# Attention scores in four 64x64 parts of the array, AV's copies on VectorE, and a replanned order

## The chip, the cores and the metric

The kernel runs on one core of one Trainium2 chip. The metric is device time in microseconds of one execution; less is better. The core's engines work from queues of their own: PE (TensorE matmuls; PEld are its weight loads), ACT (ScalarE), DVE (VectorE), POOL (GpSimd), and SP, which here only starts DMAs. They meet through semaphores.

## The reference, cut to what matters

Sliding window attention with four sink keys, 4 batches, 8 heads, 768 positions, head size 64, and behind it a mixture of experts that takes each token once:

```python
scores = q @ k.T / sqrt(64)
keep = (key < 4) | ((query - key >= 0) & (query - key < 128))
a = softmax(where(keep, scores, -1e9))
x = (a @ v)                       # [3072 tokens, 512]
# MoE: 8 experts, 384 tokens each, assigned greedily by x @ w_gate
out[tokens of e] = relu(x @ w1[e]) @ w2[e]
```

All is float32.

## The kernel before, in words

**Chunks.** Attention works in 24 chunks of 128 queries (`c`; `i = c % 6` is the block within a batch), each with all 8 heads as four pairs. The two heads of a pair lie in partitions 0 to 63 and 64 to 127 of `q` and `k`. A query sees the keys of its own block up to itself, those of the block before from itself on (exclusive), and the four sinks: 128 window keys and four sinks for every query.

**One chunk's operations** (each a function `op_...` of `attention`; a digit is the pair or the half):
- `QK0` to `QK3` (L68 to L74, PE): scores of one pair, for both heads `s`; 128 queries against 260 columns: 128 keys of the block before, the block's four sinks (copied in front of it in `kk`), 128 keys of the block. In the first block (`i = 0`) there are 132 columns, and no block before. Each float32 matmul shows in the trace as two passes.
- `cp` (L75 to L81, DVE, `copy_predicated`): overwrites the scores of the block's keys that lie behind the query with those of the block before for the same position, which are exactly the keys that the window lets through there; in the first block with -1e9. In the second block (`i = 1`) one more small copy (L80) masks sinks that are already in the window. After it, 132 columns hold all that counts.
- `mx` (L84, DVE): negated maximum over the 132 columns. `e` (L89, ACT): exponential with that bias, and its sum read out.
- `T0`, `T1` (L95, PE): transposes of the 128 window columns, `pe` (L96, ACT): copy of them to SBUF, `A`, `B` (L97, L98, POOL): the part that belongs to the block itself and to the block before.
- `ss`, `Ts`, `pS` (L100, L104, L105): the sink columns gathered, transposed, copied.
- `AV0`, `AV1` (L112, PE): values by probabilities, two pairs each, 32 instructions in a chunk (16 in a first block); both heads of a pair go to two halves of the columns of the array. `ae0`, `ae1` (L115, ACT): copies of AV from PSUM to `at`.
- `X0`, `X1` (L121, L124, PE): sinks' part, and `at` transposed back with the gate's logits beside it; `xe` (L126, DVE) scales by the sums' reciprocals (`ra`, `r`), `lm` (L128, DVE) adds the logits, `xo` (SP) stores x.

**Shapes on PE.** QK, T, Ts and X use 64 rows by 128 columns of the array (`64*128` in the trace), in two halves of the rows side by side; AV uses `128*64`, two halves of the columns.

**Buffers.** Four PSUM tiles `pp` of two banks each are shared by QK, T, Ts, AV, X; a QK's tile is free after its exponentials, AV's after both `ae`.

**What sets the order.** Nothing is scheduled on the chip. `schedule` (L220) is a list planner that runs on the host when the kernel is built: `table` gives each operation its engine, a cost in ns and its inputs; `buffers` says what must be free; `SWITCH` adds a cost when PE goes from one kind of operation to another (`c` is AV, `n` is U, `r` the rest); a priority is chunk number times a period plus the operation's `OFF`. `plan` turns the result into one sequence, and `attention` emits it in that order, so each engine's queue has that order. Loads of q and k for the chunk four ahead are started behind QK3, those of v behind QK2, the store behind `xe`, all on SP. POOL scales q (`qs`).

**Ahead and behind.** Seven matmuls on zeros (L48) warm the clock while the first loads run. After attention come routing (from L506, L530: small matmuls and DVE chains), then the expert layers; they are not touched.

Of the kernel before, what the change touches and what calls it, by code (L numbers as in the profile page):

```python
# [7 lines left out]
AF=mybir.ActivationFunctionType; OP=mybir.AluOpType; AX=mybir.AxisListType  # L8
# [7 lines left out]
def attention(ctx,tc,qd,kd,vd,vs,ud,iwd,ident,idn,x_dram,L,side={}):  # L16
# [16 lines left out]
    def T(tag,c,op=None): return R[tag][pl['slot'][tag,op or tag,c]]  # L33
# [11 lines left out]
    m1=mprev[:,0:4]  # L45

    pp=[ps.tile([128,2,512],F32,name=f"pp{j}") for j in range(bn['p'])]
    for i in range(7): PE.matmul(pp[0][:,0],wz[:,0:128],wz,start=True,stop=True)  # L48
    R.update(p=pp)

    sst=[[tl([128,2,B,HP,4],f"ss{b}_{j}") for j in range(bn['ss'])] for b in range(B)]
# [15 lines left out]
    def op_qs(c,h=slice(0,HP),e=G): e.tensor_scalar(qs[c%NQ][:,h],qs[c%NQ][:,h],0.125,None,op0=OP.mult)  # L67
    def op_QK(c,g):  # L68

        i=c%NB; q=qs[c%NQ]; sp=T('p',c,f'QK{g}')  # L70
        k0=(i-1)*W+4 if i else 0; n=260 if i else 132
        for s in range(2):
            p=slice(64*s,64*s+64)
            PE.matmul(sp[:,s,:n],q[p,g,:],kk[p,g,k0:k0+n],start=True,stop=True)  # L74
    def op_cp(c,g):  # L75

        i=c%NB; sp=T('p',c,f'QK{g}')
# [34 lines left out]
                    PE.matmul(av[64*s:64*s+64,hp-2*g,:],T('v',j)[:,h*64:h*64+64],T(x,c)[:,h,:],start=hp==2*g and x=='A',stop=x=='B' or not i,skip_group_check=True)  # L112
    def op_ra(c): V.tensor_scalar(T('r',c),T('sm',c),1e-9,None,op0=OP.add)
    def op_r(c): V.reciprocal(T('r',c),T('r',c))
    def op_ae(c,g): A.activation(T('at',c)[:,2*g:2*g+2],T('p',c,'AV0')[:,g,0:256].rearrange("p (j n)->p j n",j=2),AF.Copy)  # L115
    def op_X(c,g):

        xp=T('p',c,'X0')
# [46 lines left out]
def table(cfg):  # L165
    o={}
    def add(k,e,c,deps,alloc=()): o[k]=(e,c,deps)
    f0=lambda x: lambda c: x if c==0 else None
    f1=lambda x: lambda c: None if c==0 else x
    for p in range(3): add(f'qs.{p}','V',f0((195,195,260)[p]),[(f'ldq{p}',0)])  # L170
    add('qs','P',lambda c: 1450 if c else None,[('ldq',0)])
    for h in range(4):
        add(f'QK{h}','E',lambda c: 435 if c%NB else 225,[('ldk',0),('ldk',-1),('qs',0),(f'qs.{min(h,2)}',0),(f'ldk{min(h,2)}',0)])
        add(f'cp{h}','V',lambda c: 550 if c%NB==1 else 345,[(f'QK{h}',0)])
        add(f'mx{h}','V',344,[(f'cp{h}',0)])
        add(f'e{h}','A',697,[(f'mx{h}',0)])
    ae=[(f'e{h}',0) for h in range(4)]
    for g in range(2):
        add(f'T{g}','E',440,[(f'e{2*g}',0),(f'e{2*g+1}',0),('ldn',0)])
        add(f'pe{g}','A',479,[(f'T{g}',0)])  # L180
        add(f'A{g}','P',596,[(f'pe{g}',0)])
        add(f'B{g}','P',lambda c: 596 if c%NB else None,[(f'pe{g}',0)])
    add('zs','P',lambda c: 480 if c%NB==1 and c//NB<B-1 else None,[('A1',0)])
    add('ss','A',130,ae+[('~zs',1-NB)])
    add('ra','V',75,ae)
    add('r','V',120,[('ra',0)])
    add('Ts','E',115,[('ss',0),('ldn',0)])
    add('pS','A',230,[('Ts',0)])
    add('U','E',f0(860),[('ldu',0)])
    add('Uc','A',f0(160),[('U',0)])  # L190
    add('um','V',f0(120),[('Uc',0),('ldS',0)])
    for g in range(2):
        add(f'AV{g}','E',lambda c,g=g: 870 if c%NB else 435,
            [(f'A{g}',0),(f'B{g}',0),('ldV',0),('ldV',-1)]+([] if g==0 else [('AV0',0)]))
        add(f'ae{g}','A',285,[(f'AV{g}',0)])
    add('X0','E',950,[('ae0',0),('pS',0),('um',0),('ldi',0)])
    add('X1','E',460,[('X0',0),('ae1',0)])
    add('xe','V',680,[('X1',0),('r',0)])
    add('lm','V',135,[('xe',0)])
    add('xo','S',0,[('xe',0)])  # L200

    add('fi','P',lambda c: 500 if 2<=c<8 else None,[('A1',0)])
    last={'L':'lm'}
    for j,(cost,rd,wr) in enumerate(PREP):
        add(f'pr{j}','V',lambda c,cost=cost: cost if c==AHEAD else None,[(last[x],0) for x in rd.split() if x in last and x!='L']+([('ldn',0),('lm',-1),('lm',-2),('lm',-3)] if j==0 else []))
        last[wr]=f'pr{j}'
    return o
# [12 lines left out]
def schedule(cfg,off,T,nb=NC,dl={}):  # L220
# [63 lines left out]
    while len(out)<total:  # L284
        best=None
        for e,a in avail.items():
            cand=[]
            for p,k,c in a:
                s=max(et[e],ready[k,c]); ok=True
                for t,g in alltag.get(k,()):  # L290
                    if (t,g,c) in got: continue
                    f=free[t]
                    if not f: ok=False; break
                    if f[0][0]>s: s=f[0][0]
                if ok: cand.append((s,p,k,c))
            if not cand: continue
            m=min(cand)[0]
            x=min((p,s,k,c) for s,p,k,c in cand if s<=m+WIN)
            if best is None or x[1]<best[0]: best=(x[1],e,x[0],x[2],x[3])
        if best is None: return None  # L300
        s,e,p,k,c=best
        avail[e].remove((p,k,c))
        cost=o[k][1]; cost=cost(c) if callable(cost) else cost
        skip=cost is None
        if skip: s=ready[k,c]; t1=s
        else:
            t1=s+cost
            if e=='E':
                md='c' if k[:2]=='AV' else 'n' if k=='U' else 'r'
                t1+=SWITCH.get(mode[0]+md,0); mode[0]=md  # L310
            if e=='E' and s<60000 and s-et[e]>400:
                fr=[('p',x[1]) for x in free['p'] if x[0]<=et[e]]
                if fr: fills.append((et[e]+1,(fr[-1],int((s-et[e]-150)//(216 if et[e]>3420 else 430)))))
            if e!='S': et[e]=t1
        out.append((s,k,c,t1,skip))
        for t,g in alltag.get(k,()):
            if (t,g,c) not in got:
                got.add((t,g,c)); f=free[t]; j=0
                while j+1<len(f) and f[j+1][0]<=s: j+=1
                slot[t,g,c]=f.pop(j)[1]  # L320
        resolve(k,c,t1,skip)
        released(k,c,t1+200)
        if k=='AV1' or k[:2]=='QK':
            if c and c%NB: released(k+'+',c-1,t1+200)
            if c%NB==NB-1: released(k+'+',c,t1+200)
        if k=='xo': t=trig(t1,'xo',c); released('xod',c,dma(t+100,1456))
        if k=='QK3':
            n=c+AHD
            if n<nb:
                t=trig(t1,'ldk',n); resolve('ldk',n,dma(t,Q)); t=trig(t,'ldq',n); resolve('ldq',n,dma(t,Q))  # L330
        if k=='QK2' and c: t=trig(t1,'lv',c); resolve('ldV',c,dma(t,750))
    return max(x[3] for x in out),out,ld+[(t,'fill',f) for t,f in fills],slot
SOLO={'p'}
SWITCH=dict(rc=250,cr=200,nc=200,cn=150,nr=90,rn=200)
def plan_of(res,cfg):
    ms,out,ld,slot=res
    ev=[(s,2,k,c) for s,k,c,t,sk in out if not sk and k!='xo']+[(t,1,k,c) for t,k,c in ld]
    ev.sort(key=lambda x:x[:3])
    sl={((t,g,c) if t in SOLO else (t,t,c)):j for (t,g,c),j in slot.items()}
    return dict(seq=[(k,c) for _,_,k,c in ev],slot=sl,bufs={t:n for t,(n,_) in buffers(cfg).items()})  # L340
OFF={'A0': 117339, 'A1': -133923, 'AV0': 12422, 'AV1': -21208, 'B0': 10595, 'B1': 259267, 'QK0': -22052, 'QK1': -14777, 'QK2': -13749, 'QK3': -6157, 'T0': 4670, 'T1': -246750, 'Ts': 2621, 'U': 152873, 'Uc': -95211, 'X0': 17495, 'X1': -104106, 'ae0': 2467, 'ae1': -31194, 'cp0': 278259, 'cp1': -108689, 'cp2': 87460, 'cp3': 64960, 'e0': -138537, 'e1': -108673, 'e2': -114256, 'e3': -23766, 'fi': 109507, 'lm': -139787, 'mx0': -116627, 'mx1': -231823, 'mx2': 124490, 'mx3': 5320, 'pS': -115720, 'pe0': -173530, 'pe1': -184, 'pr0': 159594, 'pr1': -86684, 'pr10': 59638, 'pr11': -60475, 'pr12': 217358, 'pr13': -126818, 'pr14': 80178, 'pr15': 130654, 'pr2': -40108, 'pr3': -132402, 'pr4': -221748, 'pr5': 217675, 'pr6': -82969, 'pr7': 10706, 'pr8': -58787, 'pr9': 116352, 'qs': 14397, 'r': 10669, 'ra': -56880, 'ss': 189502, 'um': 89415, 'xe': 45272, 'xo': -27345, 'zs': -53942, 'pr16': 130654}
PCFG={'win': 80}
def plan():
    cfg=PCFG
    return plan_of(schedule(cfg,OFF,11557.5,dl=DL),cfg)
DL={}

I16=mybir.dt.int16; F16=mybir.dt.float16
# [7 lines left out]
class Graph:  # L356

    def __init__(self): self.t=[]; self.lw={}; self.rd={}
    def add(self,e,cost,fn,r=(),w=(),name='',cls='',lat=None):
        i=len(self.t); dep={}  # L360
        def on(j,war=False):
            if j is None: return
            pe=self.t[j][0]
            l=0 if war and pe==e else ML.get(pe+e,200) if lat is None or war else lat
            dep[j]=max(dep.get(j,0),l)
        for x in r: on(self.lw.get(x))
        for x in w:
# [440 lines left out]
```

## Time and profile before

| | |
|---|---|
| median of 3 runs | 534.67 us (530.03 to 535.22) |
| the profiled execution's own time | 532.35 us |
| its span, first to last instruction | 530.6 us |
| its mean granted TensorE clock | 0.958 of full speed |
| busy, share of the span | PE 92%, PEld 76%, DVE 66%, ACT 47%, POOL 29% |

How to read the rows below: times are us from the span's start unless said otherwise. In a timeline a row is one run of like instructions: its start, how long until the last of them ended, engine, line of the kernel, operation, output and inputs by name, partitions x elements, how many; a bracket gives idle time of the engine just before, and what ended it. A matmul's end is modelled and includes the way through the array, so starts tell more than durations: the distance between the starts of two neighbours on PE is what one costs in a stream. "Who waited for whom" puts a wait down to the releaser that came last.

### The profile page before, as it was taken

The numbers are of one execution on the slowest core, as the hardware profiler recorded it, in microseconds if no ns is written. First come the engines' busy times: TensorE is split into PE (matmuls) and PEld (weight loads), VectorE is DVE, ScalarE is ACT, GpSimd is POOL, SyncE is SP. The second block draws the span as 40 slices with busy tenths as digits, with TensorE's granted clock in tenths as the row PEclk, the third lists the DMA queues.
The fourth block names the chain that finished last, engine by engine and source line by source line (L and its number), as shares of the span: only waits on it lengthen the run. The fifth ranks groups of instructions, "written<-read, shape, count | busy, mean of one in ns | idle before, by whom it ended". The sixth has DMA issues, their size and how long they took to land. (4 is left out here: it accounts for less than half of the span.)

```text
span 530.6 us, 11127 instructions
## 1 busy us (share of the span) xinstructions
PE 487.3 (92%) x3999; PEld 404.7 (76%) x3999; DVE 350.1 (66%) x1112; ACT 248.7 (47%) x714; POOL 152.0 (29%) x207
## 2 busy tenths in 40 slices
PE   6999999999995497999989999989999989999994
PEld 4687787787873267868868977868878868999983
DVE  3766767777676686787787897877788765642100
ACT  4788887888860053153153163162055155442110
POOL 4767665665550030041032030040031041210011
PEclk8999999999997589998998999998999999999998
DMA  7566665566321171291092281380183386610001
GB/s 238 159 195 175 179 184 169 162 171 168 89 59 40 64 255 60 78 318 43 22 324 91 65 272 62 120 298 21 35 283 110 117 251 238 198 61 20 21 34 45
DMA packets 74934, 72.87 MB, mean 137 GB/s; under 512 B 28032, under 2 KB 57472, under 8 KB 74880
## 3 DMA queue, kind: packets, MB, share of 16 engines
q1 hardware_dynamic: 71040, 59.58, 36.7%
q0 software_dynamic: 3840, 12.59, 6.7%
q8 instruction: 31, 0.51, 0.4%
q14 instruction: 23, 0.19, 0.1%
HBM read 59.57 MB, written 12.58 MB: 136 GB/s over the span
## 5 line engine op out<-in xcount | busy, mean ns | idle before, releaser
L639 ACT ACTIVATE wh<-raw 128x1024 fp32r<-128x1024 f32 x64 | 67.6, 1059 | 94.9 <-DMA raw<-w 60.5
L641 DVE TENSOR_TENSOR wl<-raw,wh 128x1024 fp32r<-128x1024 f32 x64 | 77.7, 1219 | 33.2 <-ACT wh L639 32.6
L667 PE MATMUL ph<-xh,wh 128*128 128x384 f32 x256 | 92.4, 361 | 3.5 <-DVE hl L671 3.5
L667 PE MATMUL ph<-xh,wl 128*128 128x384 f32 x256 | 86.5, 338 | 0.0
L667 PE MATMUL ph<-xl,wh 128*128 128x384 f32 x256 | 86.5, 338 | 0.0
L670 ACT ACTIVATE hh<-ph 128x384 fp32r<-128x384 f32 x64 | 31.1, 489 | 104.3 <-PE ph L667 74.2
L679 PE MATMUL py<-wh,hh 128*128 128x512 f32 x192 | 79.7, 415 | 0.1
L684 POOL DMA_INDIRECT out<-yo,idx x24 | 28.5, 1189 | 176.9 <-ACT yo L682 117.3
L679 PE MATMUL py<-wh,hl 128*128 128x512 f32 x192 | 76.7, 399 | 0.4 <-DVE hl L671 0.4
L679 PE MATMUL py<-wl,hh 128*128 128x512 f32 x192 | 76.4, 398 | 0.0
L89 ACT ACTIVATE P<-pp,nmx 128x132 f32<-128x132 f32 x192 | 69.2, 369 | 9.3 <-DVE nmx L84 7.6
L646 POOL DMA_INDIRECT xg<-x_dram,idx x24 | 28.4, 1183 | 134.0 <-PE py L679 68.4
L74 PE MATMUL pp<-kk,q 64*128 64x260 f32 (+1 forms) x384 | 58.4, 403 | 1.4 <-issue 0.6
L671 DVE SCALAR_TENSOR_TENSOR hl<-ph,hh 128x384 fp32r<-128x384 f32 x64 | 35.1, 552 | 35.0 <-ACT hh L670 34.3
L667 PEld LDWEIGHTS ph<-xh,wh 128*128 128x128 f32 x256 | 49.2, 192 | 7.8 <-DVE hl L671 5.1
L79 DVE COPY_PREDICATED pp<-mprev,pp 128x256 f32<-128x256 int32 x80 | 34.0, 424 | 26.5 <-PE pp L104 16.5
L667 PEld LDWEIGHTS ph<-xl,wh 128*128 128x128 f32 x256 | 48.6, 190 | 1.8
L667 PEld LDWEIGHTS ph<-xh,wl 128*128 128x128 f32 x256 | 48.4, 189 | 0.0
L97 POOL TENSOR_SCALAR_AFFINE_SELECT A<-PT 128x512 f32<-128x512 f32 x48 | 31.1, 647 | 48.8 <-ACT PT L96 48.8
L679 PEld LDWEIGHTS py<-wh,hl 128*128 128x128 f32 x192 | 36.6, 191 | 9.0 <-DVE hl L671 0.8
L679 PEld LDWEIGHTS py<-wh,hh 128*128 128x128 f32 x192 | 37.0, 193 | 7.9 <-issue 2.7
L84 DVE TENSOR_REDUCE nmx<-pp 128x2 f32<-128x264 f32 x96 | 40.8, 429 | 1.5
(146 smaller groups left out, 843.3 us busy)
## 6 DMA issues: line engine op xcount, KB each, us to landing
raw<-w SPq DMA_DIRECT2D x64, 512.0 KB, 5.0
v<-vd SPq DMA_DIRECT2D x24, 256.0 KB, 3.6
x_dram<-xt SPq DMA_DIRECT2D x24, 256.0 KB, 3.0
kk<-kd SPq DMA_DIRECT2D x23, 264.0 KB, 3.8
q<-qd SPq DMA_DIRECT2D x23, 256.0 KB, 4.1
xg<-x_dram,idx POOLq DMA_INDIRECT x24, 4.7
out<-yo,idx POOLq DMA_INDIRECT x24, 3.2
us<-ud SPq DMA_DIRECT2D x1, 288.0 KB, 4.2
```

Of the source, the lines that this page charges most:

```text
L74: PE.matmul(sp[:,s,:n],q[p,g,:],kk[p,g,k0:k0+n],start=True,stop=True)
L79: V.copy_predicated(sp[:,:,132:260],mprev[:,None,:].to_broadcast([128,2,128]),sp[:,:,0:128])
L84: V.tensor_reduce(T('nmx',c)[:,2*g:2*g+2],sp[:,:,o:o+132],AX.X,OP.max,negate=True)
L89: A.activation(T('P',c)[:,h,:],sp[:,s,o:o+132],AF.Exp,bias=T('nmx',c)[:,h:h+1],scale=1.0,accum_out=T('sm',c)[:,h:h+1])
L97: def op_A(c,g): G.affine_select(T('A',c)[:,4*g:4*g+4],T('PT',c)[:,4*g:4*g+4],[[0,4],[1,128]],OP.is_ge,0.0,base=0,channel_multiplier=-1)
L639: g.add('A',947,lambda wh=wh,raw=raw: nc.scalar.activation(wh,raw,AF.Copy),[f'raw{n%4}'],[f'wh{s}'],f'H{k}.{j}',f'W{k}')
L641: g.add(e,{'V':1135,'P':2303}[e],lambda wh=wh,wl=wl,raw=raw,e=e: (nc.vector if e=='V' else nc.gpsimd).tensor_tensor(wl,raw,wh.bitcast(F32) ...
L667: nc.tensor.matmul(p[:,0:CAP],x[:,c,:],y[:,c,:],start=c==0 and i==0,stop=c==3 and i==2)
L670: g.add('A',371,lambda f=f,p=p: nc.scalar.activation(self.hh[:,f,:],p[:,0:CAP],AF.Relu),ps,[f'hh{f}'],f'hh{k}.{f}',f'H{k}')
L671: g.add('V',469,lambda f=f,p=p: nc.vector.scalar_tensor_tensor(self.hl[:,f,:],p[:,0:CAP],0.0,self.hh[:,f,:].bitcast(F32),op0=OP.max,op1=OP ...
L679: nc.tensor.matmul(p,x[:,f,ts],w,start=f==0 and i==0,stop=f==7 and i==2)
L684: st=nc.gpsimd.indirect_dma_start(out=self.out,out_offset=bass.IndirectOffsetOnAxis(ap=idx[:,t:t+1],axis=0),in_=y,in_offset=None)
```

## The change

Four things change. The scores of a pair are computed in two halves of the queries: queries 0 to 63 against columns 0 to 196 and queries 64 to 127 against columns 64 to 260 (in a first block 0 to 68, and 0 to 132). What is left out are keys behind every query of the half, and keys that have left the window for all of them, which `cp` overwrites or never takes. Each matmul then has 64 rows and 64 columns of the array, and the two halves and the two heads lie in four different parts. `ae` becomes a copy on VectorE. The planner's costs of QK, T, Ts, X and `ae` are new, it prices QK (`q`) as a kind of its own, and all priorities `OFF` and the period are new, so it plans another order. The warming matmuls are eight and go over all eight PSUM banks.

```diff
-    for i in range(7): PE.matmul(pp[0][:,0],wz[:,0:128],wz,start=True,stop=True)
+    for i in range(8): PE.matmul(pp[i//2][:,i%2],wz[:,0:128],wz,start=True,stop=True)
...
         k0=(i-1)*W+4 if i else 0; n=260 if i else 132
-        for s in range(2):
-            p=slice(64*s,64*s+64)
-            PE.matmul(sp[:,s,:n],q[p,g,:],kk[p,g,k0:k0+n],start=True,stop=True)
+        for h,(a,b) in enumerate(((0,n-64),(64 if i else 0,n))):
+            for s in range(2):
+                p=slice(64*s,64*s+64); r=slice(64*h,64*h+64)
+                PE.matmul(sp[r,s,a:b],q[p,g,r],kk[p,g,k0+a:k0+b],start=True,stop=True)
...
-    def op_ae(c,g): A.activation(T('at',c)[:,2*g:2*g+2],T('p',c,'AV0')[:,g,0:256].rearrange("p (j n)->p j n",j=2),AF.Copy)
+    def op_ae(c,g): V.tensor_copy(T('at',c)[:,2*g:2*g+2],T('p',c,'AV0')[:,g,0:256].rearrange("p (j n)->p j n",j=2))
...
-        add(f'QK{h}','E',lambda c: 435 if c%NB else 225,[...])
+        add(f'QK{h}','E',lambda c: 340 if c%NB else 190,[...])
-        add(f'T{g}','E',440,[...])
+        add(f'T{g}','E',350,[...])
-    add('Ts','E',115,[('ss',0),('ldn',0)])
+    add('Ts','E',65,[('ss',0),('ldn',0)])
-        add(f'ae{g}','A',285,[(f'AV{g}',0)])
-    add('X0','E',950,[...])
-    add('X1','E',460,[...])
+        add(f'ae{g}',cfg.get('ae','A'),{'A':268,'V':335}[cfg.get('ae','A')],[(f'AV{g}',0)])
+    add('X0','E',905,[...])
+    add('X1','E',420,[...])
...
-                md='c' if k[:2]=='AV' else 'n' if k=='U' else 'r'
+                md='c' if k[:2]=='AV' else 'n' if k=='U' else 'q' if k[:2]=='QK' else 'r'
...
-SWITCH=dict(rc=250,cr=200,nc=200,cn=150,nr=90,rn=200)
+SWITCH=dict(rc=60,qc=60,cr=120,cq=210,rq=105,qr=10,nc=200,cn=150,nr=90,rn=200,nq=150,qn=150)
...
-OFF={'A0': 117339, 'A1': -133923, 'AV0': 12422, ...}
-PCFG={'win': 80}
+OFF={'A0': 55242, 'A1': 26787, 'AV0': 18367, ...}
+PCFG={'win': 80, 'ae': 'V'}
...
-    return plan_of(schedule(cfg,OFF,11557.5,dl=DL),cfg)
+    return plan_of(schedule(cfg,OFF,11987.9,dl=DL),cfg)
```

## Rows read from the trace of the kernel before

**Rows 1.** The page's first part: PE's busy time, share of the span and instructions.
```profile
PE 487.3 (92%) x3999; PEld 404.7 (76%) x3999; DVE 350.1 (66%) x1112; ACT 248.7 (47%) x714; POOL 152.0 (29%) x207
```

**Rows 2.** Busy time in two stretches, attention in full flow and six of its chunks: the stretch, its length, then busy us (instructions) of PE, PEld, DVE, ACT and POOL, the granted clock, the DMA share and GB/s.
```profile
26.00:159.00 133.00, 126.78 (x1810) 106.55 (x1808) 93.81 (x280) 109.67 (x462) 79.90 (x112) 1.00 0.57 155
...
62.50:99.60 37.10, 35.38 (x506) 29.65 (x502) 26.43 (x77) 31.11 (x132) 22.76 (x31) 1.00 0.63 173
```

**Rows 3.** The timeline of PE alone, one chunk (62.59 to 68.67) and the AV six chunks later: start, duration with the last one's drain, line, output and inputs, form, how many were merged.
```profile
62.59 0.44 PE L112 MATMUL pp<-A,v 128*64 128x128 f32 x4
...
64.49 0.71 PE L74 MATMUL pp<-kk,q 64*128 64x260 f32 x4
65.03 0.22 PE L104 MATMUL pp<-idt,ss 64*128 64x64 f32 x2
65.10 0.41 PE L95 MATMUL pp<-idt,P 64*128 64x64 f32 x8
65.53 0.71 PE L74 MATMUL pp<-kk,q 64*128 64x260 f32 x4
66.07 0.65 PE L121 MATMUL pp<-vx,pS 64*128 64x288 f32 x4
66.56 1.01 PE L124 MATMUL pp<-iw,at 64*128 64x72 f32 x16
67.40 1.09 PE L74 MATMUL pp<-kk,q 64*128 64x260 f32 x8
68.33 0.41 PE L95 MATMUL pp<-idt,P 64*128 64x64 f32 x8
68.67 0.44 PE L112 MATMUL pp<-A,v 128*64 128x128 f32 x4
...
99.64 0.44 PE L112 MATMUL pp<-A,v 128*64 128x128 f32 x4
```

**Rows 4.** The same view in stretches so short that pairs of matmuls show (a stretch lists what is in flight in it): the last pair of T and the AV behind it, the last pair of an AV and the first pairs of the QK behind it, and pairs within a QK.
```profile
93.83 0.23 PE L95 MATMUL pp<-idt,P 64*128 64x64 f32 x2
93.99 1.09 PE L112 MATMUL pp<-A,v 128*64 128x128 f32 x16
...
94.80 0.28 PE L112 MATMUL pp<-A,v 128*64 128x128 f32 x2
95.01 0.49 PE L74 MATMUL pp<-kk,q 64*128 64x260 f32 x2
95.34 0.39 PE L74 MATMUL pp<-kk,q 64*128 64x260 f32 x2
...
98.64 0.82 PE L74 MATMUL pp<-kk,q 64*128 64x260 f32 x6
99.08 0.39 PE L74 MATMUL pp<-kk,q 64*128 64x260 f32 x2
```

**Rows 5.** Who waited for whom from 26 to 159 us: engine, what it was to write, line, the releaser, us in total, times, the longest.
```profile
DVE pp L79 <- PE pp L104: 16.5, 16, 1.2
...
PEld pp L95 <- ACT P L89: 8.9, 15, 0.8
...
ACT at L115 <- PE pp L112: 3.0, 7, 0.5
...
PEld pp L74 <- ACT at L115: 1.6, 10, 0.2
...
PEld pp L121 <- ACT at L115: 0.5, 3, 0.2
```

**Rows 6.** The timelines of DVE, ACT and PE around one stall, one engine after the other.
```profile
81.87 0.43 DVE L84 TENSOR_REDUCE nmx<-pp 128x2 f32<-128x264 f32 x1
...
82.08 0.20 ACT L89 ACTIVATION_READ_ACCUMULATOR P<-pp,nmx 128x1 f32 x1
82.77 0.38 ACT L115 ACTIVATE at<-pp 128x256 f32<-128x256 f32 x1 [0.50 <-PE pp L112]
83.05 0.37 ACT L89 ACTIVATE P<-pp,nmx 128x132 f32<-128x132 f32 x1
...
83.20 0.22 PE L104 MATMUL pp<-idt,ss 64*128 64x64 f32 x2
83.92 0.46 PE L95 MATMUL pp<-idt,P 64*128 64x64 f32 x8 [0.50 <-ACT P L89]
```

**Rows 7.** Groups of instructions by line and form, 26 to 159 us: busy us and mean ns of one, then idle time just before them.
```profile
L79 DVE COPY_PREDICATED pp<-mprev,pp 128x256 f32<-128x256 int32 x70 | 29.7, 424 | 23.9 <-PE pp L104 16.5 <-PE pp L74 4.6 <-ACT at L115 1.6
...
L126 DVE TENSOR_TENSOR xt<-pp,r 128x576 f32<-128x576 f32 x22 | 16.6, 757 | 10.2 <-PE pp L124 10.0
L115 ACT ACTIVATE at<-pp 128x256 f32<-128x256 f32 x44 | 15.5, 391 | 3.0 <-PE pp L112 3.0
```

**Rows 8.** The page's last part, one DMA issue: times, KB each, us from issue to landing.
```profile
q<-qd SPq DMA_DIRECT2D x23, 256.0 KB, 4.1
```

**Rows 9.** PE's timeline at the start of the kernel and where attention hands over to routing (line 506).
```profile
0.84 3.14 PE L48 MATMUL pp<-const-float32-0.0 128*128 128x512 bf16 x7 [0.84 <-PEq L801]
3.92 1.33 PE L74 MATMUL pp<-kk,q 64*128 64x132 f32 x8
...
5.77 0.72 PE L74 MATMUL pp<-kk,q 64*128 64x132 f32 x8 [0.20 <-DVE q L67]
...
163.18 0.48 PE L506 MATMUL pr<-grid,onesb 128*128 128x384 bf16 x2 [0.86 <-DVE xt L126]
```

More of the change, by code (lines that the diff above doesn't have):

```diff
@@ L172, in table @@
     for h in range(4):
-        add(f'QK{h}','E',lambda c: 435 if c%NB else 225,[('ldk',0),('ldk',-1),('qs',0),(f'qs.{min(h,2)}',0),(f'ldk{min(h,2)}',0)])
+        add(f'QK{h}','E',lambda c: 340 if c%NB else 190,[('ldk',0),('ldk',-1),('qs',0),(f'qs.{min(h,2)}',0),(f'ldk{min(h,2)}',0)])
         add(f'cp{h}','V',lambda c: 550 if c%NB==1 else 345,[(f'QK{h}',0)])
@@ L178, in table @@
     for g in range(2):
-        add(f'T{g}','E',440,[(f'e{2*g}',0),(f'e{2*g+1}',0),('ldn',0)])
+        add(f'T{g}','E',350,[(f'e{2*g}',0),(f'e{2*g+1}',0),('ldn',0)])
         add(f'pe{g}','A',479,[(f'T{g}',0)])
@@ L194, in table @@
             [(f'A{g}',0),(f'B{g}',0),('ldV',0),('ldV',-1)]+([] if g==0 else [('AV0',0)]))
-        add(f'ae{g}','A',285,[(f'AV{g}',0)])
-    add('X0','E',950,[('ae0',0),('pS',0),('um',0),('ldi',0)])
-    add('X1','E',460,[('X0',0),('ae1',0)])
+        add(f'ae{g}',cfg.get('ae','A'),{'A':268,'V':335}[cfg.get('ae','A')],[(f'AV{g}',0)])
+    add('X0','E',905,[('ae0',0),('pS',0),('um',0),('ldi',0)])
+    add('X1','E',420,[('X0',0),('ae1',0)])
     add('xe','V',680,[('X1',0),('r',0)])
@@ L340, in plan_of @@
     return dict(seq=[(k,c) for _,_,k,c in ev],slot=sl,bufs={t:n for t,(n,_) in buffers(cfg).items()})
-OFF={'A0': 117339, 'A1': -133923, 'AV0': 12422, 'AV1': -21208, 'B0': 10595, 'B1': 259267, 'QK0': -22052, 'QK1': -14777, 'QK2': -13749, 'QK3': -6157, 'T0': 4670, 'T1': -246750, 'Ts': 2621, 'U': 152873, 'Uc': -95211, 'X0': 17495, 'X1': -104106, 'ae0': 2467, 'ae1': -31194, 'cp0': 278259, 'cp1': -108689, 'cp2': 87460, 'cp3': 64960, 'e0': -138537, 'e1': -108673, 'e2': -114256, 'e3': -23766, 'fi': 109507, 'lm': -139787, 'mx0': -116627, 'mx1': -231823, 'mx2': 124490, 'mx3': 5320, 'pS': -115720, 'pe0': -173530, 'pe1': -184, 'pr0': 159594, 'pr1': -86684, 'pr10': 59638, 'pr11': -60475, 'pr12': 217358, 'pr13': -126818, 'pr14': 80178, 'pr15': 130654, 'pr2': -40108, 'pr3': -132402, 'pr4': -221748, 'pr5': 217675, 'pr6': -82969, 'pr7': 10706, 'pr8': -58787, 'pr9': 116352, 'qs': 14397, 'r': 10669, 'ra': -56880, 'ss': 189502, 'um': 89415, 'xe': 45272, 'xo': -27345, 'zs': -53942, 'pr16': 130654}
-PCFG={'win': 80}
+OFF={'A0': 55242, 'A1': 26787, 'AV0': 18367, 'AV1': -22083, 'B0': 278983, 'B1': 205348, 'QK0': -27720, 'QK1': -26311, 'QK2': -12010, 'QK3': -4988, 'T0': 8014, 'T1': -135681, 'Ts': 4632, 'U': 28397, 'Uc': -86089, 'X0': 20369, 'X1': -130490, 'ae0': 53040, 'ae1': -33379, 'cp0': 440348, 'cp1': -192187, 'cp2': 171248, 'cp3': 7562, 'e0': -89532, 'e1': -287293, 'e2': -241651, 'e3': -78722, 'fi': 142969, 'lm': -133651, 'mx0': -248907, 'mx1': -145333, 'mx2': 240344, 'mx3': -7150, 'pS': -119032, 'pe0': -212135, 'pe1': 19659, 'pr0': 195376, 'pr1': 59384, 'pr10': -138939, 'pr11': -113681, 'pr12': 255698, 'pr13': -275309, 'pr14': 141817, 'pr15': 661, 'pr16': -48149, 'pr2': -52279, 'pr3': -86569, 'pr4': -280403, 'pr5': 200454, 'pr6': -19483, 'pr7': -68686, 'pr8': -99028, 'pr9': 275771, 'qs': -96066, 'r': -136243, 'ra': -3122, 'ss': 170779, 'um': 320156, 'xe': 57870, 'xo': 4402, 'zs': -27092}
+PCFG={'win': 80, 'ae': 'V'}
 def plan():
     cfg=PCFG
-    return plan_of(schedule(cfg,OFF,11557.5,dl=DL),cfg)
+    return plan_of(schedule(cfg,OFF,11987.9,dl=DL),cfg)
 DL={}
```

## The prediction

> **What bounds the kernel now.** I read the page's busy shares first, then the stages, then one chunk of attention instruction by instruction, then the waits, because the change touches attention alone.
>
> The page gives PE 92% of the span [rows 1], but that mixes three stages: attention, routing, expert layers. The stage table [rows 2] shows attention in full flow from 26 to 159 us, at the full granted clock (1.00): PE is busy 126.8 of 133.0 us, ACT 109.7, DVE 93.8, POOL 79.9. Routing's first matmul starts at 163.18 [rows 9]; nothing behind it is edited. So only the first 163 us can move, and what is won there is kept only if it ends the last chunk of attention earlier.
>
> One chunk on PE [rows 3]: from the AV that starts at 62.59 to the next at 68.67 is 6.08 us, and the starts add up: AV 1.90, QK 0.54, Ts 0.07, T 0.43 (its own 0.34 and a short wait of the QK behind it), QK 0.54, X's first part 0.49 and second 0.84, two QK together 0.93, T 0.34. Six chunks (62.59 to 99.64) take 37.05 us, 6.18 each, although one of the six, the first block of a batch, has half an AV and scores of 132 columns. So PE is the bound in quiet chunks, and there are waits in others.
>
> The waits [rows 5] name these: weight loads of T stood 8.9 us for ACT's exponentials, those of QK 1.6 us and of X 0.5 us for ACT's copies of AV (`ae`). ACT itself stood seven times, 3.0 us, in front of `ae` until AV ended. One such stall [rows 6] shows what this does. ACT is free at 82.28 and the next exponential has had its maximum since 82.30 (81.87 + 0.43), but `ae0` is ahead of it in ACT's queue and starts only at 82.77 when AV is done; the exponentials come at 83.05 and later, and T starts 0.72 us after Ts (83.20, 83.92) instead of 0.07 (65.03, 65.10).
>
> **The change part by part.** Durations are of the profiled execution: 532.35 us, span 530.6, 1.75 around it; it is 0.4% under the median of the runs (534.67, from 530.03 to 535.22). I add to 532.35.
>
> *AV's copies to DVE.* 48 copies of 128x256 leave ACT, where one takes 391 ns [rows 7]. On DVE no such copy is in the trace; the nearest rows are 424 ns for a predicated copy of the same 128x256 and 757 ns for 128x576 [rows 7], which bound it by about 0.3 and 0.45 us. DVE would carry some 0.85 us more of 6.18 us per chunk. Cover: DVE stood 16.5 us, 16 times, up to 1.2 us each, for the QK behind AV [rows 5], which is when the copies fall due. An `ae` that waits on DVE now holds the predicated copy and the maximum queued behind it, 0.77 us of work for the next exponential; that is the price if the cover is gone.
> What goes: the seven stalls of 0.65 us (0.72 - 0.07), 4.5 us; next late is the same pair of exponentials by its own length (82.30 plus two of 0.37 plus 0.2 for the read of its sum [rows 6], 83.2), which leaves about 0.1 us each, so 3.9; the 1.6 and 0.5 us that QK and X stood for `ae` on ACT also go, since DVE is idle when AV ends. Together 6.0 us. Bounds: at best all of T's waits, 8.9 + 1.6 + 0.5 = 11.0; at worst seven holds of 0.77 come back on DVE and nothing is won, +5.4. I take -6.0.
>
> *The scores.* A QK is two passes per head, the two heads of a pair side by side; a pass slot of 260 columns takes 0.22 us (98.64 to 99.08 is two of them) [rows 4]. Now each head's queries are halved and each half asks for 196 columns: 0.22 x 196/260 = 0.166 us, if the four 64x64 parts run side by side. The trace shows two row halves side by side (QK) and two column halves (AV), not four. The instructions double to eight matmuls and eight loads: T issues eight with their loads in 0.34 us, X sixteen in 0.84 (eight in 0.42) [rows 3], so a QK lies between 0.33 and its present 0.44. I take 0.33, because T's loads are longer than the new ones and still keep that pace. Gain per QK 0.108, per chunk 0.43, over 20 chunks 8.6 us; the four first-block chunks gain nothing, because the second half still asks for all 132 columns. Bounds 0 and -8.6.
>
> *The price of a new shape.* QK, T, Ts and X all ran in 64x128 parts; only AV (128x64) differed. The trace shows a change of shape [rows 4]: T to AV, 0.16 us from the last pair to the first (93.83, 93.99), where pairs of T come 0.06 apart: +0.10. AV to QK, 0.21 (94.80, 95.01) against 0.11: +0.10, and the first slot takes 0.33 (95.01, 95.34) where a QK behind X loses 0.05 of its 0.22 (four slots in 0.93): +0.06 more, 0.16. Now each group of QKs is a shape of its own. With three groups in a chunk as now [rows 3] there are five new changes, with two groups three, with QKs one by one seven. The diff's planner charges them and will group; I take four, between 0 (a change that leaves two row halves in place might not drain) and 0.16, at 0.08, close under the lower row because the row split stays: 24 x 4 x 0.08 = 7.7 us. Bounds: 24 x 3 x 0 = 0 and 24 x 7 x 0.16 = 27 us.
> The Trainium skill, TensorEngine Tiling (Array Packing), section Key Properties, says that changing the tiling mode drains the engine, while going to another tile of one mode does not. The trace agrees for AV [rows 4]; no row shows 64x64 against 64x128. By that rule the change to 64x64 costs like AV's, and the sum would be that of rival A below.
> The same skill, TensorE: Matmul & The Clock Gate, Part 3, gives about 4 ns per extra tile for tiles that run together; by it, as an estimate, a QK would be 0.35 us. No run here shows four.
>
> *The order.* The planner's costs, its prices of a shape change and all priorities are new, so the sequence on every engine is another. The instructions are as many on POOL and SP; loads of q, k and v hang on QK2 and QK3 as before, four chunks (some 24 us) ahead, and land in about 4 us [rows 8], which hides their move. I cost the order itself at nothing beyond the terms above: it may remove more waits, or add some; the bounds of the first term hold both.
>
> *The start.* One more clock warming matmul: seven took 3.14 us [rows 9], so one is 0.45. The first QKs start at 3.92, behind the warming, but the later ones wait for a scaled piece of q until 5.77 [rows 9], which hides it; +0.45 if not.
>
> Sum: 532.35 - 6.0 - 8.6 + 7.7 = 525.45, **525.5 us**.
>
> **Rivals.**
> *A, the shape changes eat it.* Place: each border between QK and T, Ts or X. Price 0.16 as for AV to QK, five to seven per chunk: 24 x (5 to 7) x 0.16 = 19 to 27 us, less 8.6 and 6.0: 537 to 545, about 541. It is slower than before once changes times price exceed 14.6/24 = 0.61 us per chunk (0.12 each with five). For it: both rows of AV. Against it: the row split stays.
> *B, only two parts run together.* Then a QK is four slots of 0.166, 0.66 instead of 0.44: +17.9 over 80 QKs, +7.7 - 6.0: 552. For it: no row has four. Against: both halves separately do it.
> *C, the waits move.* The copies on DVE hold the maxima, or PE waits for the four PSUM tiles that scores, T, AV and X share; the 6.0 do not come: 531.5, up to 535. For it: DVE goes from 26.4 of 37.1 us in six chunks [rows 2] to some 31.5 of 36 with twelve copies of 0.42. Against: its hole lies where the copies fall.
> *D, the shapes change nearly free* (0.02, 1.9 us) *and T's other waits go as well* (3 us more of the 8.9): 532.35 - 8.6 + 1.9 - 9 = 516.7.
>
> **How the numbers follow.** The forecast has 0.40 (its own range 519 to 531), A 0.20, B 0.06, C 0.22, D 0.12. About 1% is what a measurement of this kernel can tell from no change: under 529.3 or over 540. Faster: 0.38 of the forecast, D, and 0.05 of C, 0.55. Same: 0.02 of the forecast, 0.16 of C, 0.09 of A, 0.27. Slower: 0.11 of A, B, 0.01 of C, 0.18. The range runs from 515 (below D) to 541 (the middle of A); B and the upper half of A stay outside.
>
> **What would show it.** Right: QK slots of about 0.166 us with four matmuls starting within some 20 ns; quiet chunks of about 5.9 us or less; ACT no longer idle before `ae`, T following Ts within 0.2 us; routing's first matmul some 7 us before 163. Wrong: pairs of QK matmuls a slot apart (B); 0.15 us and more between the last QK and the first T, or before QK, wherever shapes meet (A); DVE waiting for AV while maxima are due, or QK waiting for a PSUM tile (C). The expert layers should keep their time; if they don't, the sum was made in the wrong place.

## The result, and the profile after

The changed kernel is slower, a little: 533.11 us (median of 20 runs, 529.95 to 539.21) against 531.34 for the kernel before (20 runs, 527.12 to 535.27) run beside it; the ratio is 1.0072, 95% interval 1.0049 to 1.0096. The ratio is taken over the executions in the fast state alone; the quotient of the two medians of all executions is 1.0033. The profiled execution took 537.36 us, span 535.7, where that of before took 532.35. The forecast was 525.5 and 55% for faster: wrong in sign. Lines of attention are two further down than before (QK L76, T L97, `e` L91, Ts L106, AV L114, `ae` L117, X L123 and L126, `xe` L128, routing L508).

The page's first part, which answers to [rows 1]: 385 more matmuls, 4.1 us more of PE.

```profile
PE 491.4 (92%) x4384; PEld 395.6 (74%) x4384; DVE 374.6 (70%) x1160; ACT 237.2 (44%) x666; POOL 156.6 (29%) x207
```

The stretch of [rows 2] after the change, same columns: ACT has 10 us less and DVE 20 more, but PE, the bound, has 129.73 us instead of 126.78 in the same 133 us.

```profile
26.00:159.00 133.00, 129.73 (x2106) 96.41 (x2105) 113.71 (x317) 99.50 (x417) 79.44 (x110) 1.00 0.55 152
```

PE's timeline, answering to [rows 3] and [rows 9]: one chunk and the handover to routing. The first QK starts at 4.34 for 3.92, and routing at 168.11 for 163.18, so attention ends 4.9 us later. The chunk takes 6.20 us (66.69 to 72.89) for 6.08. The QK's own shrank: two together take 0.84 (71.85 to 72.69), 0.93 before. What lies behind a QK grew: X's first part 0.59 (70.08 to 70.67) for 0.49, a T between two QKs 0.50 (69.08 to 69.58) for 0.43; 0.18 of this 0.50 is a wait of the QK behind it for the new copies.

```profile
66.69 0.44 PE L114 MATMUL pp<-A,v 128*64 128x128 f32 x4
...
68.59 0.56 PE L76 MATMUL pp<-kk,q 64*64 64x196 f32 x8
69.08 0.46 PE L97 MATMUL pp<-idt,P 64*128 64x64 f32 x8
69.58 0.56 PE L76 MATMUL pp<-kk,q 64*64 64x196 f32 x8
70.08 0.76 PE L123 MATMUL pp<-vx,pS 64*128 64x288 f32 x4
70.67 1.01 PE L126 MATMUL pp<-iw,at 64*128 64x72 f32 x16
...
71.85 0.90 PE L76 MATMUL pp<-kk,q 64*64 64x196 f32 x16
72.69 0.28 PE L106 MATMUL pp<-idt,ss 64*128 64x64 f32 x2
72.89 0.33 PE L114 MATMUL pp<-A,v 128*64 128x128 f32 x2
...
168.11 0.32 PE L508 MATMUL pr<-grid,onesb 128*128 128x384 bf16 x1 [0.86 <-DVE xt L128]
```

The same view in very short stretches, answering to [rows 4]. Four matmuls are in one slot, so the four parts do run side by side (their starts are 7 ns apart). The last two slots before 72.41 take 0.33 together, 0.166 each. But the last slot lasts 0.28 (72.41 to the Ts at 72.69 above), 0.11 more than its neighbours, and the first of a group 0.22.

```profile
68.59 0.40 PE L76 MATMUL pp<-kk,q 64*64 64x196 f32 x4
68.80 0.35 PE L76 MATMUL pp<-kk,q 64*64 64x196 f32 x4
...
72.08 0.68 PE L76 MATMUL pp<-kk,q 64*64 64x196 f32 x11
72.41 0.35 PE L76 MATMUL pp<-kk,q 64*64 64x196 f32 x4
```

Who waited for whom from 26 to 159 us, answering to [rows 5]. T's loads waited 8.9 us for the exponentials before; that is 0.3 now. In its place T's and X's loads stand 6.8 and 3.7 us for nothing that the profile shows ("issue"), and QK waits for the new copies (3.8). DVE stands 10.9 us in front of a copy until AV ends; before, it stood 16.5 us at about the same place for the QK behind AV [rows 5]. ACT waits 11.2 us for maxima, 7.4 before.

```profile
ACT P L91 <- DVE nmx L86: 11.2, 25, 1.7
DVE at L117 <- PE pp L114: 10.9, 17, 1.0
PEld pp L97 <- issue: 6.8, 26, 0.3
...
PEld pp L76 <- DVE at L117: 3.8, 16, 0.5
PEld pp L123 <- issue: 3.7, 14, 0.3
...
PEld pp L97 <- ACT P L91: 0.3, 1, 0.3
```

### The profile page after: what moved, and what is told of

Same layout as the page of the kernel before. It is cut to its first block, busy times and chain, and to the rows that moved or that the text cites. A ratio compares the mean times of both kernels' runs of the same rounds, so it can differ in the third digit from the quotient of the medians.

```text
span 535.7 us, 11908 instructions
## 1 busy us (share of the span) xinstructions
PE 491.4 (92%) x4384; PEld 395.6 (74%) x4384; DVE 374.6 (70%) x1160; ACT 237.2 (44%) x666; POOL 156.6 (29%) x207
## 5 line engine op out<-in xcount | busy, mean ns | idle before, releaser
L686 POOL DMA_INDIRECT out<-yo,idx x24 | 31.1, 1295 | 174.1 <-ACT yo L684 142.1
L91 ACT ACTIVATE P<-pp,nmx 128x132 f32<-128x132 f32 x192 | 68.9, 366 | 15.3 <-DVE nmx L86 12.5
L76 PE MATMUL pp<-kk,q 64*64 64x196 f32 (+2 forms) x768 | 52.7, 359 | 3.5 <-DVE pp L81 1.2
L681 PEld LDWEIGHTS py<-wl,hh 128*128 128x128 f32 x192 | 36.6, 191 | 4.4
```

The lines of the kernel that those rows point to most:

```text
L76: PE.matmul(sp[r,s,a:b],q[p,g,r],kk[p,g,k0+a:k0+b],start=True,stop=True)
L91: A.activation(T('P',c)[:,h,:],sp[:,s,o:o+132],AF.Exp,bias=T('nmx',c)[:,h:h+1],scale=1.0,accum_out=T('sm',c)[:,h:h+1])
L681: nc.tensor.matmul(p,x[:,f,ts],w,start=f==0 and i==0,stop=f==7 and i==2)
L686: st=nc.gpsimd.indirect_dma_start(out=self.out,out_offset=bass.IndirectOffsetOnAxis(ap=idx[:,t:t+1],axis=0),in_=y,in_offset=None)
```

## The experiments

Ratios are to the kernel before on the same chip, with 95% intervals. Single executions differ in the expert stage, which nothing here edits: from its first matmul to the end it took 327.6 to 335.9 us in the profiled executions. So, beside the ratio, traces are compared inside attention: by the AV of chunk 7, by the twelve chunks from there to chunk 19 (74.08 us before), and by routing's first matmul (163.18 before).

### The parts one by one

The copies alone, in the order of before, twice (`d_only`, `d_again`):

```diff
-    def op_ae(c,g): A.activation(T('at',c)[...],...,AF.Copy)
+    def op_ae(c,g): V.tensor_copy(T('at',c)[...],...)
```

> The kernel before with one edit: ae on VectorE; scores and emitted order as before. Theory 1 (shape changes between 64x128 and 64x64 ate the gain, the copies' move did win): the seven stalls of T behind Ts (4.0 us in twelve chunks) go, 3 to 6 us faster than before, ratio 0.989 to 0.995. Rival 2 (the copies on VectorE hold its queue and cost as much as they free): ratio 0.998 to 1.006, with QK or the maxima waiting for ae. Rival 3 (the late clock at the start makes the loss): the clock is back at 2.4 GHz near 15 us as before.

> The kernel before with ae on VectorE alone, once more, beside the next kernel. Theory 1 (waits come back elsewhere, and at the end the copies of the last chunks queue on VectorE behind routing's preparation): steady stage as before within 0.3 us in twelve chunks, 29.8 us instead of 26.5 from chunk 19's AV to routing, ratio 1.000 to 1.007.

531.39 us, ratio 1.0002 (0.9972 to 1.0032), and 532.46, 1.0012 (0.9969 to 1.0055). Twelve chunks took 73.86 and 73.87 us: 0.2 less, not the 3 that half of the 6.0 would be: rival 2's range, not theory 1's. PE's weight loads waited from 26 to 159 us 18.9 us in all, against 19.0 before. The rows of `d_only` show the exchange: T's wait for exponentials, 8.9 in [rows 5], is still 6.9, and X waits 2.2 us for copies instead of 0.5.

```profile
PEld pp L95 <- ACT P L89: 6.9, 14, 0.9
...
PEld pp L121 <- DVE at L115: 2.2, 4, 0.5
```

The stalls did go, but not every one was worth its length. The distances from AV to AV, by the block that the first of the two AVs belongs to (in the twelve chunks there are two of each kind):

| block | 1 | 2 | 3 | 4 | 5 | 0 (first) |
|---|---|---|---|---|---|---|
| before, us | 6.07 | 6.07 | 6.02 | 6.36 | 6.87 | 5.65 |
| `d_only`, us | 5.96, 5.97 | 6.18, 5.96 | 6.30, 5.84 | 6.50, 6.77 | 6.17, 6.16 | 6.03, 6.03 |

The stall stood in blocks 4 and 5. Block 5 gains its 0.7. Block 4, the chunk of [rows 6], gains nothing, and the timelines of before and of `d_only` show why. Before:

```profile
82.66 0.71 PE L74 MATMUL pp<-kk,q 64*128 64x260 f32 x4
...
83.48 0.43 DVE L79 COPY_PREDICATED pp<-mprev,pp 128x256 f32<-128x256 int32 x1 [1.18 <-PE pp L104]
...
86.78 0.41 PE L95 MATMUL pp<-idt,P 64*128 64x64 f32 x8
```

`d_only`, DVE, ACT and PE one after the other, and PE at the end of attention:

```profile
83.45 0.75 DVE L115 COPY at<-pp 128x256 f32<-128x256 f32 x2 [0.40 <-PE pp L112]
84.15 0.43 DVE L79 COPY_PREDICATED pp<-mprev,pp 128x256 f32<-128x256 int32 x1
...
85.71 0.37 ACT L89 ACTIVATE P<-pp,nmx 128x132 f32<-128x132 f32 x1 [0.60 <-DVE nmx L84]
...
83.33 0.71 PE L74 MATMUL pp<-kk,q 64*128 64x260 f32 x4
83.87 0.22 PE L104 MATMUL pp<-idt,ss 64*128 64x64 f32 x2
83.95 0.46 PE L95 MATMUL pp<-idt,P 64*128 64x64 f32 x8
...
87.53 0.47 PE L95 MATMUL pp<-idt,P 64*128 64x64 f32 x8 [0.24 <-ACT P L89]
...
156.60 0.46 PE L95 MATMUL pp<-idt,P 64*128 64x64 f32 x8 [1.45 <-DVE xt L126]
```

T now follows Ts after 0.08 (83.87, 83.95) instead of 0.72. But the second T behind this AV waits for exponentials whose maximum stands in DVE's queue behind the masking and the maximum of the QK behind AV, and this chain is as long as it was: from that QK to the second T 4.12 us before (82.66 to 86.78), 4.20 now (83.33 to 87.53). Before, the last of these exponentials ended at 86.61 (the read of its sum at 86.41 takes 0.20), so the second T could have come at most 0.17 earlier, and most of the 0.65 was slack. The copies don't hold the masking: it starts 0.82 us behind the start of its QK in both (82.66 and 83.48, 83.33 and 84.15), and the two copies fill the hole in which DVE stood 1.18 us before. Behind the AV of a first block they do cost: there one copy stands behind a masking in DVE's queue and the other behind a maximum too (96.29 and 96.96), X waits for them, and the distance is 0.38 longer.

At the end of attention DVE's queue also holds routing's preparation, and PE stands 1.45 us for `xe`. Routing starts at 164.92 in `d_again` and at 166.66 in `d_only`. Most of the 1.7 between the two is the clock: in `d_only` it was granted at 1.2 GHz from 157.9 to 161.3, where four matmuls of AV took 0.65 us and not 0.39, in `d_again` at 2.4.

The same with the last four chunks' copies left on ACT (`d20`):

```diff
+    def op_ae(c,g):
+        if c<20: V.tensor_copy(...)
+        else: A.activation(...,AF.Copy)
```

> As the one before, but the last four chunks keep ae on ACT. Theory 1: the end of attention takes 26.5 us again and 3.3 us come back against the copies' move for all chunks; ratio to the kernel before 0.995 to 1.001. If the end's 3.3 us have another cause, 29 to 30 us stay there.

531.69 us, ratio 1.0011 (0.9975 to 1.0046); twelve chunks take 73.88, and routing starts at 163.23 (26.40 us from chunk 19's AV, as expected), so the loss at the end is gone, and what is left of the copies is nothing.

The scores alone, in the order of before (`s_only`; the diff's loop over halves and its eight warming matmuls):

> The kernel before with one edit: scores by halves of the queries in 64x64 parts (with the eight warming matmuls that go with it); ae on ACT, emitted order as before. Theory 1: QK slots 0.166 us, each exit from QK 0.25 and more, each entry 0.15 to 0.20; five new changes a chunk cost some 0.63 us against 0.48 gained, 3 to 6 us slower than before, ratio 1.005 to 1.012. Rival 3 (late clock): the start is as before, the gain of the slots shows, ratio 0.990 to 0.998.

532.76 us, ratio 1.0034 (1.0001 to 1.0068), slower as theory 1 has it but by less than the 1.005 expected; twelve chunks 75.21 us, routing at 165.99. PE's timeline of the chunk of [rows 3]: the four QKs take 1.81 us (0.49, 0.50 and 0.82) instead of 2.01, which is 0.20 less and not 0.43. The rest but AV takes 2.41 instead of 2.17: Ts +0.05, X's parts +0.09 and +0.11, the second T +0.05, and only the first T is shorter, since the QK behind it waited before. The chunk, 6.12, is 0.04 longer than 6.08. Over the twelve chunks, by PE's starts, the QKs take 2.5 us less than before, X's two parts 2.4 more, T 0.8 and Ts 0.5 more.

```profile
66.11 0.56 PE L76 MATMUL pp<-kk,q 64*64 64x196 f32 x8
66.60 0.28 PE L106 MATMUL pp<-idt,ss 64*128 64x64 f32 x2
66.72 0.41 PE L97 MATMUL pp<-idt,P 64*128 64x64 f32 x8
67.09 0.56 PE L76 MATMUL pp<-kk,q 64*64 64x196 f32 x8
67.59 0.76 PE L123 MATMUL pp<-vx,pS 64*128 64x288 f32 x4
68.17 1.01 PE L126 MATMUL pp<-iw,at 64*128 64x72 f32 x16
69.12 0.90 PE L76 MATMUL pp<-kk,q 64*64 64x196 f32 x16
69.94 0.46 PE L97 MATMUL pp<-idt,P 64*128 64x64 f32 x8
70.33 0.33 PE L114 MATMUL pp<-A,v 128*64 128x128 f32 x2
```

Both in the order of before (`sd`):

> The kernel before with scores in 64x64 parts and ae on VectorE, emitted order as before. Theory 1, with the copies' move worth nothing because the waits come back elsewhere: as with the scores alone, ratio 1.000 to 1.008. Rival 2 (copies on VectorE cost): 1.008 or more. If the two edits help one another (slower PE, so DVE's hole is wider): under 1.000.

533.06 us, ratio 1.0043 (1.0007 to 1.0080). Twelve chunks 73.62, less than either part alone; the end of attention gives it back (29.68 us from chunk 19's AV to routing, 26.51 before; here too the clock was at 1.2 GHz for a part of it, from 159.0 to 162.4).

The changed order alone, with whole scores and copies on ACT (`o_only`), and with whole scores but copies on DVE (`do`):

> The kernel before with the changed kernel's emitted order alone; scores whole in 64x128, ae on ACT. Theory 1: no shape is new, so PE needs no more than before; the order was planned for ae on VectorE, so ACT waits for AV in front of ae; ratio 0.998 to 1.012. Rival 3 (late clock by this order): the clock comes back only near 25 us and the first AV starts about 3 us later than at 19.1; ratio 1.005 or more.

> The changed kernel with scores whole in 64x128 as before (seven warming matmuls); ae on VectorE and the new order stay. Theory 1 (five changes of shape a chunk at about 0.14 us cost more than the 0.43 us the shorter scores give): without them the changed kernel gets 2 to 6 us back, ratio to the kernel before 0.997 to 1.005. Rival 5 (the new order itself is the loss): it stays slow, ratio 1.008 or more, and six chunks take over 37.5 us with PE waiting for exponentials or PSUM tiles.

`o_only`: 544.35 us, ratio 1.0255 (1.0206 to 1.0304), a miss: this order was planned for copies on DVE, and with them on ACT a chunk is half a microsecond longer (80.43 in twelve). `do` tells more: 533.36 us, ratio 1.0051 (1.0012 to 1.0091). Its twelve chunks take 74.12, as before, and its end 26.34; but the AV of chunk 7 comes at 65.23 instead of 62.59. The 2.6 us are lost while the pipeline fills. PE's timeline of `do` there: QK waits 1.23 us, and a T and two more QKs go ahead of the first AV, at 22.35. The row puts the wait down to a masking on DVE. A QK also needs a PSUM tile that exponentials have freed, and a pair of them ends at 19.48; which of the two it was is not shown.

```profile
16.23 2.12 PE L74 MATMUL pp<-kk,q 64*128 64x260 f32 x12 [0.37 <-ACT pS L105]
19.57 0.71 PE L74 MATMUL pp<-kk,q 64*128 64x260 f32 x4 [1.23 <-DVE pp L79]
...
20.94 1.41 PE L74 MATMUL pp<-kk,q 64*128 64x260 f32 x8 [0.24 <-ACT P L89]
22.35 1.10 PE L112 MATMUL pp<-A,v 128*64 128x128 f32 x16
```

In the same view of before, one QK goes ahead of the AV at 19.08, after a wait of 0.34:

```profile
15.89 2.14 PE L74 MATMUL pp<-kk,q 64*128 64x260 f32 x12 [0.42 <-issue]
18.37 0.71 PE L74 MATMUL pp<-kk,q 64*128 64x260 f32 x4 [0.34 <-ACT P L89]
19.08 1.09 PE L112 MATMUL pp<-A,v 128*64 128x128 f32 x16
```

The clock does not explain this loss. The granted clock was at the lower of its two levels, 1.2 GHz, behind the first QKs, and back at 2.4 GHz at 15.2 us before and at 16.1 in `do`. The twelve QK records at 15.89 and 16.23 run at the same pace in both and start 0.34 apart; the first AVs behind them are 3.27 apart. In `o_only` the first AV comes at 22.49, so the loss does not hang on which engine copies. (The rows of `o_only` show a clock of 1.00 throughout, but its T and twelve QK records before 16 us last 0.69 and 2.92 us, as those of `do` do at 1.2 GHz, so they can't be used for this.)

With the shorter scores the clock came back later in six of seven traces, at 21.8 to 25.7 us, against 15.2 to 17.9 in five with whole scores; why is not shown. `after` and `after_again` (25.7 and 24.0) have their first AV where `do` has it (22.40 and 22.05), but take 6.76 and 6.59 us from there to the second, where `do` takes 5.83. So 0.8 to 0.9 us of what the scores cost at routing falls in this stretch.

> The changed kernel once more, for a second look at its start and a closer interval. Rival 3 as a property of the order: clock back near 25 us again, first AV at about 22.4. If it is chance from run to run: back near 15 us, first AV near 19 to 20, and this profiled execution is some 3 us shorter than the first one's 537.4. Theory 1: the steady stage takes 37.5 us for six chunks either way, ratio 1.005 to 1.010 overall.

535.23 us, ratio 1.0091 (1.0056 to 1.0126): the late clock and the late first AV came again; chunk 7 at 66.18, twelve chunks 75.07, routing at 167.71. Against `do` (165.69) the scores cost 2.0 us here and 2.4 in the first trace of the changed kernel; `s_only` against before, 2.8.

### Is it the border between shapes?

X in 64x64 as well, beside the scores (`s_x64`), or alone with whole scores (`x_only`). The second part of X is split in the same way:

```diff
+            for r in (slice(0,64),slice(64,128)):
                 for s in range(2):
-                    ...; PE.matmul(xp[:,s,0:288],T('pS',c)[p],vx[p],...)
+                    ...; PE.matmul(xp[r,s,0:288],T('pS',c)[p,r],vx[p],...)
```

> The kernel before (ae on ACT, its order) with scores in 64x64 parts and X too, by halves of the queries. New changes of shape a chunk fall from five to three, and X's sixteen matmuls, bound by loads of 128 columns at 0.112 us a pair, have loads of 64. Theory 1: 0.28 us from two changes and some 0.3 to 0.4 from X against the scores alone, PE some 0.5 us a chunk shorter than before; as waits refill part of it, ratio 0.980 to 0.995. Rival 6 (waits on exponentials and PSUM tiles bound the stage, PE's sum doesn't): ratio 0.996 to 1.004.

> The kernel before with X by halves of the queries in 64x64 parts, scores whole in 64x128. A test of the price of a shape without the shorter scores: two new changes a chunk (QK to X and X to QK) at about 0.14 us, 0.28, against some 0.1 us that X itself is shorter. Theory 1: 0.15 to 0.2 us a chunk longer on PE, ratio 1.002 to 1.008, with about 0.256 less slot at the exit and 0.09 more at each border. If the price belongs to the short scores and not to the shape: faster than before, 0.990 to 0.998.

`s_x64`: 528.0 us, ratio 0.9977 (0.9941 to 1.0013), twelve chunks 72.43: less than theory 1's 0.980 to 0.995, and in rival 6's range. `x_only`: 527.29 us, ratio 0.9959 (0.9926 to 0.9992), twelve chunks 72.90: a miss, slower was expected. The border costs what it should: QK to X's first part takes 0.64 (65.05 to 65.69) where [rows 3] have 0.54, and X's first part 0.53 for 0.49. But X's second part takes 0.61 (66.22 to 66.83) for 0.84. Its eight slots, each with a load, go from 0.112 us to 0.062. At the pace of a QK's slot, 72 columns cost 0.061 (0.22 x 72/260), so they now go at the pace of their columns; before, with loads of 128 columns (188 ns each, 133 now), it was most likely the load that held them. For `x_only` I had put X's gain at 0.1 us.

```profile
65.05 0.71 PE L74 MATMUL pp<-kk,q 64*128 64x260 f32 x4
65.69 0.71 PE L122 MATMUL pp<-vx,pS 64*64 64x288 f32 x8
66.22 0.68 PE L126 MATMUL pp<-iw,at 64*64 64x72 f32 x32
66.83 1.15 PE L74 MATMUL pp<-kk,q 64*128 64x260 f32 x8
```

T and Ts in 64x64 too, so that only AV has another shape (`all64`; products with the identity in place of transposes):

```diff
-                PE.transpose(t[:,s,64*j:64*j+64],T('P',c)[p,4*g+j,4:132],idn[...])
+            for h in range(2): ...
+                PE.matmul(t[64*h:64*h+64,s,64*j:64*j+64],T('P',c)[p,4*g+j,4+64*h:68+64*h],idn[...],...)
```

> As the one before, with T and Ts in 64x64 parts too, as matmuls with the identity in two passes in place of transposes, so that no shape but AV's differs, as in the kernel before. Theory 1: entries and exits between QK, T, Ts and X cost 0.05 or less each (0.166 us after the last slot of a QK, not 0.256); T grows from 0.31 to some 0.5 us, PE a little shorter in sum than with X alone, ratio 0.980 to 1.000. If the border costs stay although the shape is the same, theory 1 is wrong about their cause.

538.88 us, ratio 1.0139 (1.0087 to 1.0191), slower than expected, because the T's slots double (two passes each): by PE's starts T takes 15.0 us in twelve chunks, 9.2 in `s_x64`. The borders are what it was run for, and in PE's timeline they are gone: QK behind AV takes 0.38 (67.29 to 67.67) where after has 0.49, QK behind T 0.33 (68.28 to 68.61), which is two slots of 0.166 and nothing else, and X's first part 0.49 again (68.61 to 69.10).

```profile
67.29 0.56 PE L76 MATMUL pp<-kk,q 64*64 64x196 f32 x8
67.67 0.33 PE L108 MATMUL pp<-idt,ss 64*64 64x64 f32 x8
...
68.28 0.51 PE L76 MATMUL pp<-kk,q 64*64 64x196 f32 x8
68.61 0.66 PE L126 MATMUL pp<-vx,pS 64*64 64x288 f32 x8
69.10 0.68 PE L130 MATMUL pp<-iw,at 64*64 64x72 f32 x32
```

### A version that beats both

Scores and X in 64x64, copies on DVE for the first twenty chunks, the order of before (`x64_d20`: the edits of `s_x64` and `d20` together):

> Scores and X in 64x64 parts, ae on VectorE for the first twenty chunks, the order of the kernel before: the version that the runs so far point to. Theory 1: three new changes of shape a chunk, X shorter, waits for ACT's exponentials fewer, the end as before; attention ends at 159 to 160.5 us, ratio 0.990 to 0.998. Rival 6 (waits bound the stage): no better than scores and X alone, 0.998 or more.

525.83 us, ratio 0.9882 (0.9818 to 0.9945), twelve chunks 70.57. Here the copies are worth 1.9 us in twelve chunks (72.43 in `s_x64`), with the same order and the same copies that were worth 0.2 in `d_only`. Block 5 gains 0.7 a chunk as there; the chunk of the first block, which lost 0.38 there, loses nothing here. From 151.9 to 155.3, near the end of attention, the clock was at 1.2 GHz; routing starts at 159.80 all the same (160.42 in `s_x64`). Whether it is faster than `x_only` is not clear of noise.

## Why the prediction was wrong

What it said of the bound held: PE sets the pace in the quiet chunks, waits do in others, and only the end of attention counts. Its terms, by where routing starts or by twelve chunks doubled:

| term | predicted, us | measured, us | from |
|---|---|---|---|
| copies to DVE | -6.0 | -0.4 in 24 chunks; at routing +1.7 and +3.5 (the latter with the low clock), 0.0 with the last four chunks on ACT | `d_only`, `d_again`, `d20` |
| scores, fewer columns | -8.6 | slot 0.166, as predicted | after, `s_only` |
| price of the shape | +7.7 | about +10.9 | `s_only` |
| order | 0 | +2.5 at routing together with the copies; +2.6 by chunk 7 | `do` |
| start | 0 | no sign of one at the first AV: 19.5 in `s_only`, 19.3 to 19.8 in the copies' runs, 19.1 before | `s_only`, `d_only`, `d_again`, `d20` |
| sum | -6.9 | -8.6 + 10.9 + 2.5 = +4.8 | +4.9 and +4.5 at routing (after, `after_again`) |

The price: 20 of 24 chunks should win 0.43, in twelve chunks ten do, 4.3 us; `s_only` lost 1.1, so the changes cost 5.4 in twelve chunks, 0.45 a chunk, 10.9 in 24. At routing the scores' net is 2.0 to 2.8 (`do` against the two traces of the changed kernel, before against `s_only`), which would make the price 10.6 to 11.4.

How close the sum comes is in part its making: `do` has two of the terms in one. The loss at the fill is the order's, since `o_only`, with copies on ACT, has it too. The copies' loss at the end does not show in `do` (26.34, 28.19 in `d_again`), so the new order seems to avoid it; beside `d_again` it costs 0.8 at routing, not 2.5.

**The step that failed first is the copies' -6.0.** That ACT stood behind `ae` was right, and the stall that was shown did go. But its removal was counted as time off the end, at its own length less 0.1, because the next late input was looked for among the exponentials of the same T alone. In block 4 the next one was an input of the second T, at most 0.17 us early: its exponentials hang on the QK behind AV over DVE's queue, a chain of 4.12 us before and 4.20 in `d_only` that the copies' move does not shorten. So of the stalls (six in that stretch, three of each block; ACT's seventh wait, at 157.22, stands in front of no T) only those of block 5 were worth their 0.7, and the first-block chunks, where X waits for copies that stand behind maxima in DVE's queue, and the end of attention took that back. Rival C gave 531.5 for "the 6.0 do not come", and they did not; its first reason, that the copies hold the maxima, is not what these chunks show, and "its hole lies where the copies fall" was right.
`x64_d20` shows the other side: in `s_x64` PE is busy 122.5 of the 133 us instead of 126.8, and T's loads wait 16.4 us for exponentials (29 times); there the same copies take this to 11.1 us and win.

**The price of the shape was mis-sized, in count and in cost.** I took four changes at 0.08. There are five new ones in a chunk, three out of QK and two into it, and they come to 0.45, 0.09 each net of waits that were there before; single borders show more, up to rival A's 0.16 and beyond: the last slot of a QK +0.11, X's first part behind it +0.10, X to QK +0.10 (0.11 to 0.21). The reason that I gave for the lower value, that the row split stays, is refuted: keeping the two row halves gives no discount, and `all64` shows that the cost goes when the shape is the same. One reading of [rows 4] was also wrong: the first slot of 0.33 behind AV is not AV's price, since [rows 3] have the same 0.54 for a QK behind T (65.53); the changed QK's first slot is 0.22 behind AV and T alike.
The Trainium skill's rule that a change of the tiling mode drains the engine while another tile of the same mode does not (TensorEngine Tiling (Array Packing), Key Properties), which the prediction weighed and discounted, agrees with these runs: 0.28 for the last slot before a change, 0.166 where there is none.

**The order's 0 was wrong by 2.6 us at the fill.** I looked at the steady chunks only, and there it held (74.12 for 74.08). A replanned list also has a beginning: more QKs go ahead of the first AV, one of them waits 1.23 us where 0.34 was lost before, and the AVs behind them come 2.6 us later; how the 2.6 divides between the wait and the changed order of QK and AV is not shown. No step of the prediction looked at the stretch up to the first AV.

What stays open: why the first slot of a QK was long (0.32) in the 64x128 shape, why the clock comes back later with the shorter scores, and why the expert stage takes 327.6 to 335.9 us.

## What to carry to other kernels

Work taken off an engine that only stands in another's way is worth something only after the next late input on the same path is named and shown to be early; here it was the chain behind AV's QK, at most 0.17 us ahead of its use. Count every border where an instruction's array shape changes, in and out (here about 0.1 us each), and weigh whether all of a group's neighbours can take the new shape, as X could. A new order is costed at the fill and at the end as well as in the steady part.

## What the runs showed of the hardware

- Four 64x64 parts with four different weights and moving data run side by side, their starts 7 ns apart. The Trainium skill (TensorE: Matmul & The Clock Gate, Part 3) has about 4 ns for one more tile; for this kernel either is small beside 166.
- X's slots of 72 columns took 0.112 us with loads of 128 columns and 0.062 with loads of 64, although there are twice as many instructions. T's transposes, with loads of 128 columns that take 138 ns and not 188, kept 0.06 all along.
- Going between 64x128 and 64x64 (the same rows, half the columns) costs about as much as going between 64x128 and AV's 128x64: 0.11 on the last slot here, 0.10 at each of the two borders in [rows 4].
